# A spectral mixer and a gated feed-forward on one core: the first batch's weight preparation is paced and placed anew

## The chip, the cores and the metric

The kernel runs on one core of a Trainium2 chip. The metric is the device time of one launch in microseconds (us); lower is better. Engines are named as in the profile: PE (matmul), PEld (its weight load), DVE (VectorE), ACT (ScalarE), POOL (GpSimd) and SP (SyncE, which here only issues DMAs).

## What is computed

The input x is (8, 3008, 256). Each batch is filtered along the sequence in the frequency domain and then goes through a gated feed-forward of width 1536.

```python
X = np.fft.rfft(x, axis=1)
Y = X * (filt_r + 1j * filt_i)[None]
y = np.fft.irfft(Y, n=3008, axis=1).reshape(8 * 3008, 256)
g = y @ w_gate
out = (g / (1 + np.exp(-g)) * (y @ w_val)) @ w_out
```

All of it is float32; the gate, value and output weights arrive as float64 and are rounded to float32 on the chip.

## The kernel before

**Spectral part.** The transforms are done as matmuls with tables in stages 1, 2a, 2b and 3, 47 x 64 points at a time. For the first batch all of stages 1 and 2 and the first part of stage 3 run ahead of the feed-forward; for each later batch they run as pieces between the feed-forward's matmuls of the batch before it.

**Feed-forward.** A batch has 8 chunks of tokens (k) and 3 groups of the hidden width (g), so 24 steps. In the first batch the first nine steps go through chunks 0 to 2 for group 0 (steps 0 to 2), then for group 1 (steps 3 to 5), then for group 2 (steps 6 to 8). A fast multiplication scheme works on four blocks: instead of 32 products of blocks, a step has 26. It needs, beside the plain weights P and Q of each block, combined weights A, B and E for each pair of blocks, and sums of the sequence y for distances d = 1, 2, 3 between the blocks (tile `y_t`, function `combine_sequence`). The products land in PSUM as k (L731, tile wk), a and e (wa, we). ACT and DVE turn them into f, c, x, y, m, s, e and h (L746 to L778); POOL forms D = f - f for pairs (L228) and, one step later, sums of h (tokens S). The projections W1 to W7 (L810) of the step before run between the products; o (L225 on DVE, L821 on ACT) adds them up. All three chunks' y are summed for d = 2, 1 and 3 at tokens n2, n1 and n3 of the step before (n3 in the next step).

**Order.** The order is written out by hand: `SCHEDULE` is a list of 150 tokens that each step walks through. The place of a token in it is used in what follows; a step takes about 33 us in the first batch, so a place is worth 0.22 us. Some of the places: S00 and S01 at 5 and 6, x03 20, S10 19, S11 21, s13 22, P0 27, D01 30, A13 31, s01 43, W6 44, D02 48, D12 51, A01 52, c2 53, m01 57, x02 61, W7 62, B01 67, Q3 76, A02 80, A12 87, A23 109, n2 110, E23 123, B23 134, E03 138, n1 139, B03 142. The program keeps this order on each engine (`pin`), and each engine works strictly in its order.

**Preparation of weights.** The class `Preparation` rounds the weights in the first batch. They come as 36 halves, 12 for each group: 8 for the hidden width ("hid") and 4 for the projection ("proj"); halves 8 to 11 are the first group's projection. `round_half` makes nine stages of each: L302, L305, L317 and L321 on DVE, L307 to L314 on ACT, and on POOL a multiplication (L329 for proj, L341 and L342 for hid) and some sums. `combine_weights` makes the combined weights of one pair of blocks in three stages: a sum on DVE (L225, or L232 for d = 1), a scaling on ACT (L363, for d > 1), and then B on POOL (L228) and E on DVE (L225).

Each stage has a tick. Half i starts at tick b, 4 ticks after half i - 1, except half 8, which starts 12 ticks after half 7:

```python
                b = base[-1] + (4 if i != 2 * len(BLOCKS) else 12) if i else 0
                for n, t in enumerate((0, 1, 2, 3, 4, 6, 7, 9, 10)):
                    put(b + t, go, by, n > 6)
```

The combinations follow the last hid half of a group from tick b + 11 on, a pair a tick. Ticks 0 to 28 fall into the spectral part of the first batch. Then `preparation.finish(0)` runs those that step 0 needs, up to tick 44. After that a step runs `TICKS` ticks, evenly spread over its places; step 0 starts behind the token P0. With 22 ticks, step 0 runs ticks 45 to 62, step 1 63 to 84 and step 2 85 to 103. Rounded weights of group 0 go to `wt_t`, of group 1 to `lent`, of group 2 to `wt_t` again.

Ahead of the feed-forward PE runs filler matmuls (`idle`, L463); the last of them read the weights A13 and A01, so they, and with them stage 3 of the first chunk (L639) and step 0, wait for these.

**Other queues.** SP issues the loads of raw weights (L285), of x, t4 and tables (L478), the stores of sums and of y (L937, L934) and the weights' store to DRAM (L371), in the program's order.

Of the kernel before, what the change touches and what calls it, by code (L numbers as in the profile page):

```python
# [84 lines left out]
SCHEDULE = """  # L85
# [14 lines left out]
BLOCKS = (0, 1, 3, 2)  # L100
PAIRS = ((0, 1), (1, 2), (2, 3), (0, 2), (1, 3), (0, 3))
PAIRS_USED = ((1, 3), (0, 1), (0, 2), (1, 2), (2, 3), (0, 3))
# [3 lines left out]
SLOT = {p: i for i, p in enumerate(ORDER)}  # L106
# [38 lines left out]
def kernel(  # L145
# [10 lines left out]
    nc = tc.nc  # L156
# [36 lines left out]
    def weights_of(b, k, g):  # L193
        return wt_1 if b == 0 and k < NT and g == 1 else wt_t
# [27 lines left out]
    pin = tc.keep_in_program_order  # L222

    def add(eng, dst, a, b):
        return eng.tensor_tensor(out=dst, in0=a, in1=b, op=ALU.add)  # L225
# [125 lines left out]
    def combine_weights(g, i, j):  # L351

        d = j - i
        wt_f = weights_of(0, 0, g).rearrange("p s z f -> p s (z f)")
        m = wt_f[:, SLOT[f"A{i}{j}"]]
        ui, uj, yi, yj = [wt_f[:, SLOT[f"{p}{q}"]] for p in "PQ" for q in (i, j)]
        if d == 1:
            pin(negated_sum(m, ui, uj))
        else:
            pin(add(nc.vector, m, ui, uj))  # L360
        yield
        if d > 1:
            pin(nc.scalar.mul(m, m, -1.0 / d))  # L363
        yield
        pin(sub(nc.gpsimd, wt_f[:, SLOT[f"B{i}{j}"]], yi, m))
        pin(add(nc.vector, wt_f[:, SLOT[f"E{i}{j}"]], yj, m))

    def keep_weights(g, piece):

# [7 lines left out]
    class Preparation:  # L377
# [3 lines left out]
        def __init__(self):  # L381
            self.at, self.held = 0, []

            self.ticks, self.need = {}, {}
            base, ready = [], {}

            def put(t, f, by, pool=False):
                self.ticks.setdefault(t, ([], []))[pool].append(f)
                self.need[by] = max(self.need.get(by, 0), t)

            for i, (_, (use, *at)) in enumerate(weights):
                hid, g = use == "hid", at[0] if use == "hid" else at[0] // JB
                by = ((0, 3, 6) if hid else (1, 4, 7))[g]
                b = base[-1] + (4 if i != 2 * len(BLOCKS) else 12) if i else 0
                if i >= N_EARLY:
                    same = [n for n in range(N_EARLY, i) if spot_of(n) == spot_of(i)]
                    k = 2 if spot_of(i) is None else 1
                    last = base[same[-k]] + 8 if same[k - 1:] else 0
                    b = max(b, last + 8)
                    put(max(last, b - 10), lambda i=i: load_weights(i), by)  # L400
                base.append(b)
                if hid and g == NG - 1:
                    ready.setdefault(NT, b)
                half = []

                def go(half=half, i=i):
                    if not half:
                        half.append(round_half(i))
                    next(half[0], None)

                for n, t in enumerate((0, 1, 2, 3, 4, 6, 7, 9, 10)):
                    put(b + t, go, by, n > 6)
                if hid and at[1:] == [BLOCKS[-1], 1]:
                    for n, pair in enumerate(PAIRS_USED):
                        c = combine_weights(g, *pair)
                        for t in range(3):

                            put(b + 11 + n + t, lambda c=c: next(c, None),
                                by if g or n < 4 else 1, t == 2)
            self.barriers = sorted((t, step) for step, t in ready.items())  # L420
            self.end = max(self.ticks)
# [25 lines left out]
                self.tick(step)  # L447

    preparation = Preparation()
    TICKS = 22  # L450

# [385 lines left out]
    with tc.tile_pool(name="start", bufs=1) as spool0:  # L839
# [47 lines left out]
        for u in range(N_TWO + lag):  # L887
            if u < N_TWO:
                spec.turn(u + 2)
                step = spec.stage2a(u)  # L890
# [90 lines left out]
    def chore(step, token, f, *args):  # L981
        chores.setdefault((step, token), []).append((f, args))

    chore(0, "A01", lambda: combine_sequence(cur.y[0], 3))
    for step in range(NT):
        for d, token in ((2, "Q2"), (1, "A01"), (3, "Q3")):
            chore(step, token, keep_sums, step, d)
# [13 lines left out]
    for b in range(B):  # L1001
        cur, nxt = spec, following if b + 1 < B else None
        spec, following = nxt, Spectral(b + 2)
        plan = [[] for _ in range(NCHUNK * NG)]

        def three(s, k, cur=cur):
            return [s.stage3(k, step) for step in range(4)]

        d = [three(cur, k) for k in range(1, NCHUNK)]
        one = [nxt.stage1(u) for u in range(N_ONE)] if nxt else []  # L1010
        two = []
        for u in range(N_TWO + 2) if nxt else ():
            two += [nxt.stage2b(u - 2)] if u > 1 else []
            two += [nxt.stage2a(u)] if u < N_TWO else []
        if nxt:
            plan[0] = one[0:2] + d[0][0:1] + one[2:3] + d[0][1:2]
            plan[1] = one[3:4] + d[0][2:3] + one[4:5] + d[0][3:4] + one[5:6]
            plan[2], plan[3] = one[6:11], one[11:16]
            plan[4] = d[1] + two[0:1]

            plan[5], plan[6] = [iter(())] + two[1:5], two[5:10]
            plan[7] = two[10:11] + d[2]
            plan[8], plan[9] = two[11:16], two[16:21]
            plan[10], plan[11] = two[21:24], three(nxt, 0)
            if b == 0:
                for k in range(NCHUNK - 1):
                    plan[k] = d[k] + one[k:k + 1]
                plan[3], plan[4], plan[5] = one[3:8], one[8:13], one[13:16]
                for n in range(5):
                    plan[6 + n] = two[5 * n:5 * n + 5]  # L1030
                plan[6][0] = sooner(plan[6][0])
        else:
            plan[1], plan[4], plan[7] = d

        for step in range(NCHUNK * NG + (b == B - 1)):
            ghost = step == NCHUNK * NG
            k, g = order_of(b)[min(step, NCHUNK * NG - 1)]
            this = None
            pieces = []
            if not ghost:  # L1040
                pieces = plan[step]
                this = Group(b, k, g, cur.y[k], sequence_of(cur, nxt, step))
                if b == 0:
                    preparation.finish(step)
                chunk = {0: 1, 2: 2, 5: 3}.get(step)
                if b and chunk:
                    for i in range(2):
                        cur.load_t4(chunk, i)
            elif before is None:
                break  # L1050
            ends = {ORDER[e - 1]: n for n, (_, e) in enumerate(PIECES)}
            last = ghost or b == B - 1 and step == NCHUNK * NG - 1
            for place, token in enumerate(SCHEDULE):
                if b == 0 and this and place * TICKS % len(SCHEDULE) < TICKS and \
                        (step or place > SCHEDULE.index("P0")):
                    preparation.tick(step)
                old = token.endswith("'")
                op = token.rstrip("'")
                if op[0] == "t":
                    n = int(op[1])  # L1060
                    ps = pieces_before if old else pieces
                    if n < len(ps):
                        next(ps[n], None)
                elif op[0] in "Wo" or op.endswith(".o"):

                    g0 = older if old else before
                    if g0 is not None and (old or not ghost):
                        g0.project(op)
                else:
                    g0 = before if old else this  # L1070
                    if g0 is not None and not (ghost and op[0] == "S"):
                        g0.step(op)
                if old or this is None:
                    continue
                if nxt and (step, op) == ((4, "P2") if b else (5, "A23")):
                    nxt.load_two(0)
                if b + 2 < B and (step, op) == (9, "B01"):
                    for u in range(2):
                        following.load_x(u)
                if nxt and (step, op) == (10, "A12" if b else "E23"):  # L1080
                    for i in range(2):
                        nxt.load_t4(0, i)
                for f, args in chores.get((step, op), ()) if b == 0 else ():
                    f(*args)
                if op in ends and not last and (b or step >= NT * NG - 1):
                    reload_weights((g + 1) % NG, ends[op])
            older, before, pieces_before = before, this, pieces
# [33 lines left out]
```

## Time and profile before

| | |
|---|---|
| median of 7 runs | 2958.5 us (2957.56 to 2965.78) |
| profiled execution | 2965.28 us, its span 2963.4 us |
| busy: PE, PEld | 99%, 95% of the span |
| busy: DVE, ACT, POOL | 65%, 54%, 53% |
| mean granted clock of TensorE | 0.994 |
| first feed-forward matmul (wk, L731) | at 83.58 us |

The profile's rows are of one execution. PE's share counts a matmul as busy from start to end, so a 99% does not say that it runs at its pace; the number of matmuls (in brackets behind the busy time) in a stretch does, beside the granted clock. A wait is put down to what ended last by the profile.

### The profile page before, as it was taken

The numbers are of one execution on the slowest core, as the hardware profiler recorded it, in microseconds if no ns is written. First come the engines' busy times: TensorE is split into PE (matmuls) and PEld (weight loads), VectorE is DVE, ScalarE is ACT, GpSimd is POOL, SyncE is SP. The second block draws the span as 40 slices with busy tenths as digits, with TensorE's granted clock in tenths as the row PEclk, the third lists the DMA queues.
The fourth block names the chain that finished last, engine by engine and source line by source line (L and its number), as shares of the span: only waits on it lengthen the run. The fifth ranks groups of instructions, "written<-read, shape, count | busy, mean of one in ns | idle before, by whom it ended". The sixth has DMA issues, their size and how long they took to land.

```text
span 2963.4 us, 57624 instructions
## 1 busy us (share of the span) xinstructions
PE 2925.7 (99%) x20264; PEld 2827.8 (95%) x20264; DVE 1932.6 (65%) x4398; ACT 1613.5 (54%) x4208; POOL 1571.0 (53%) x1745
## 2 busy tenths in 40 slices
PE   8999999999999999999999999999999999999999
PEld 6888999999999999999999999999999999999999
DVE  6788765576655766557765567656676566766665
ACT  5765555555555555555555554555555555555554
POOL 3776464555445564446554555544564545555453
PEclk9899999999999999999999999999999999999999
DMA  8577865566555655557555566455665565644442
GB/s 228 179 248 247 279 218 164 186 211 193 176 182 182 220 182 175 188 182 223 184 173 180 185 208 208 156 189 185 201 204 165 182 204 189 206 140 149 147 131 89
DMA packets 217452, 558.57 MB, mean 188 GB/s; under 512 B 29962, under 2 KB 107642, under 8 KB 217166
## 3 DMA queue, kind: packets, MB, share of 16 engines
q1 hardware_dynamic: 171326, 485.59, 52.2%
q10 hardware_dynamic: 36912, 45.43, 4.5%
q0 software_dynamic: 8928, 23.89, 2.3%
q8 instruction: 162, 2.65, 0.4%
q14 instruction: 124, 1.02, 0.1%
HBM read 459.73 MB, written 95.05 MB: 187 GB/s over the span
## 4 chain that ended last, share of the span: by engine, by line
PE 93%; POOL 1%; DVE 1%; ACT 0%; issue 0%; DMA 0%; SPq 0%; POOLq 0%; DVEq 0%; ACTq 0%
PE wa L731 24%; PE wA L810 17%; PE wk L731 16%; PE we L731 12%; PE wG L810 9%; PE wF L810 4%; PE pd L639 3%; PE pa L547 3%; PE pc L619 2%; PE pb L587 2%; POOL y_t L225 1%; POOL h L228 0%; POOL D L228 0%; DMA lent<-in_filt_r_dram 0%; POOL h L225 0%
## 5 line engine op out<-in xcount | busy, mean ns | idle before, releaser
L731 PE MATMUL wa<-y_t,wt_t 128*128 128x188 f32 x4464 | 883.3, 324 | 9.6 <-ACT m L766 3.2
L731 PEld LDWEIGHTS wa<-y_t,wt_t 128*128 128x128 f32 x4464 | 732.4, 191 | 36.1 <-issue 14.7
L225 POOL TENSOR_TENSOR h<-h 128x376 f32<-128x376 f32 x190 | 183.2, 985 | 783.5 <-DVE h L778 783.5
L810 PE MATMUL wA<-wo_t,h 128*128 128x128 f32 x4608 | 577.7, 275 | 2.1 <-DVE o L225 2.1
L810 PEld LDWEIGHTS wA<-wo_t,h 128*128 128x128 f32 x4608 | 563.0, 192 | 15.6 <-issue 11.0
L731 PE MATMUL wk<-y,wt_t 128*128 128x188 f32 x2976 | 568.6, 324 | 0.2 <-ACT f L746 0.2
L228 POOL TENSOR_TENSOR h<-h 128x376 f32<-128x376 f32 x570 | 555.1, 996 | 0.5
L731 PEld LDWEIGHTS wk<-y,wt_t 128*128 128x128 f32 x2976 | 479.8, 191 | 26.6 <-issue 20.8
L228 DVE TENSOR_TENSOR we<-we,m 128x376 f32<-128x376 f32 x576 | 319.0, 556 | 198.4 <-PE we L731 140.8
L731 PE MATMUL we<-y_t,wt_t 128*128 128x188 f32 x2232 | 432.3, 323 | 1.8 <-DVE we L232 1.8
L731 PEld LDWEIGHTS we<-y_t,wt_t 128*128 128x128 f32 x2232 | 369.9, 190 | 2.5 <-DVE we L232 2.2
L228 POOL TENSOR_TENSOR D<-f,f 128x376 f32<-128x376 f32 x288 | 281.0, 989 | 107.2 <-ACT f L746 105.3
L232 DVE SCALAR_TENSOR_TENSOR y<-wk,c 128x376 f32<-128x376 f32 x480 | 245.2, 543 | 135.5 <-ACT we L762 85.0
L766 ACT COPY m<-wa 128x376 f32<-128x376 f32 x576 | 272.2, 473 | 92.2 <-PE wa L731 90.9
L773 ACT ACTIVATE g<-wa 128x188 f32<-128x188 f32 x576 | 188.2, 327 | 192.1 <-PE wa L731 184.0
L810 PE MATMUL wG<-wo_t,h 128*128 128x128 f32 x2304 | 289.5, 276 | 0.6 <-DVE o L225 0.6
L810 PEld LDWEIGHTS wG<-wo_t,h 128*128 128x128 f32 x2304 | 282.7, 192 | 0.8 <-DVE o L225 0.8
L773 ACT ACTIVATE u<-we 128x188 f32<-128x188 f32 x576 | 189.2, 329 | 167.6 <-DVE we L228 148.2
L746 ACT ACTIVATE f<-wk 128x376 f32<-128x376 f32 x288 | 139.4, 484 | 240.5 <-PE wk L731 212.5
L750 ACT COPY c<-wk 128x376 f32<-128x376 f32 x288 | 136.2, 473 | 225.6 <-PE wk L731 225.3
L753 DVE SCALAR_TENSOR_TENSOR x<-wk,f 128x376 f32<-128x376 f32 x192 | 104.5, 545 | 234.5 <-PE wk L731 230.2
L762 ACT COPY we<-y 128x376 f32<-128x376 f32 x480 | 223.5, 486 | 31.0 <-DVE h L778 12.3
(142 smaller groups left out, 3922.2 us busy)
## 6 DMA issues: line engine op xcount, KB each, us to landing
wt_t<-w_all SPq DMA_DIRECT2D x174, 896.0 KB
wt_t<-w_all SPq DMA_DIRECT2D x174, 768.0 KB
t<-d SPq DMA_DIRECT2D x62, 384.0 KB
d<-t ACTq DMA_DIRECT2D x112, 192.0 KB
lent<-de_tbl SPq DMA_DIRECT2D x84, 256.0 KB
lent<-in_filt_r_dram SPq DMA_DIRECT2D x336, 64.0 KB
lent<-d SPq DMA_DIRECT2D x84, 256.0 KB
d<-lent ACTq DMA_DIRECT2D x84, 256.0 KB
```

What stands on the lines that cost most here:

```text
L225: return eng.tensor_tensor(out=dst, in0=a, in1=b, op=ALU.add)
L228: return eng.tensor_tensor(out=dst, in0=a, in1=b, op=ALU.subtract)
L232: return nc.vector.scalar_tensor_tensor(out=dst, in0=a, scalar=-1.0, in1=b, op0=ALU.mult, op1=ALU.subtract)
L547: pin(nc.tensor.matmul(out=ps[0:NK], lhsT=wf_t, rhs=self.x.pop(u), start=True, stop=True))
L731: pin(nc.tensor.matmul(out=ps[:, z], lhsT=self.wt[:, SLOT[p], z], rhs=rhs, start=start and z == 0, stop=True, skip_group_check=True))
L746: pin(act.mul(self.small(f"f{i}", f"f{i}", 1), t[f"k{i}"], -1.0))
L750: pin(act.copy(out=self.small(f"c{i}", f"c{i}", 1), in_=t[f"k{i}"]))
L753: pin(v.scalar_tensor_tensor(out=dst, in0=t[f"k{j}"], scalar=-1.0, in1=t[f"f{i}" if j == 3 else f"D{at}"], op0=ALU.mult, op1=ALU.add))
L762: pin(act.copy(out=self.bank(f"e{at}"), in_=t[f"y{at}"]))
L766: pin(act.copy(out=self.small(f"m{at}", "m", 4), in_=t[f"a{at}"]))
L773: pin(act.activation(out=self.small(op, "g", 3, 1)[:, 0], in_=ps[:, 1], func=AF.Silu))
L810: pin(nc.tensor.matmul(out=self.tiles[at][:, t, :], lhsT=self.hs[i][:, HID[p], t0:t0 + 128], rhs=wo_t[:, JB * q + i, WO[p], :], start=star ...
```

## The change

Five places change, and all of them act on the first batch alone:

- the sum that makes E runs on DVE only for the first four pairs of group 0, which are those made ahead of the feed-forward; for the other two pairs of group 0 and for all six of groups 1 and 2 it runs on POOL, behind the same pair's B;
- half 8 starts 8 ticks after half 7 instead of 12, and all later halves 4 ticks nearer with it;
- a step runs 20 ticks instead of 22;
- in step 0 the ticks start behind A01 instead of P0;
- the sums of the sequence for d = 3 of the first chunk are made behind B01 instead of A01.

With this, step 0 runs ticks 45 to 57 (tick 58 is run by `finish` as step 1 begins), step 1 ticks 59 to 78, step 2 ticks 79 to 98. The combinations of group 1 (ticks 91 to 98) stand at places 90 to 143 of step 2, where before (95 to 102) they stood at 69 to 116. Those of group 2 (139 to 146) stand at places 0 to 53 of step 5, where before (143 to 150) they stood at place 116 of step 4 to place 14 of step 5.

```diff
         pin(sub(nc.gpsimd, wt_f[:, SLOT[f"B{i}{j}"]], yi, m))
-        pin(add(nc.vector, wt_f[:, SLOT[f"E{i}{j}"]], yj, m))
+        early = g == 0 and PAIRS_USED.index((i, j)) < 4
+        pin(add(nc.vector if early else nc.gpsimd, wt_f[:, SLOT[f"E{i}{j}"]], yj, m))
...
-                b = base[-1] + (4 if i != 2 * len(BLOCKS) else 12) if i else 0
+                b = base[-1] + (4 if i != 2 * len(BLOCKS) else 8) if i else 0
...
-    TICKS = 22
+    TICKS = 20
...
-    chore(0, "A01", lambda: combine_sequence(cur.y[0], 3))
+    chore(0, "B01", lambda: combine_sequence(cur.y[0], 3))
...
                 if b == 0 and this and place * TICKS % len(SCHEDULE) < TICKS and \
-                        (step or place > SCHEDULE.index("P0")):
+                        (step or place > SCHEDULE.index("A01")):
                     preparation.tick(step)
```

## The prediction

> **What bounds the kernel now.** I read the page's busy rows first, then the stretches by engine, then the waits of the stretches that stand out, then their instructions in order of time.
>
> ```profile
> span 2963.4 us, 57624 instructions
> PE 2925.7 (99%) x20264; PEld 2827.8 (95%) x20264; DVE 1932.6 (65%) x4398; ACT 1613.5 (54%) x4208; POOL 1571.0 (53%) x1745
> ```
>
> TensorE is busy 99% of the span: nothing on another engine counts unless it makes PE wait or its clock drop. So I look for the places where PE is not at its pace. In the stretches the columns are length, then busy us (instructions) of PE, PEld, DVE, ACT, POOL, then granted clock, DMA share, GB/s.
>
> ```profile
> 72.70:86.40 13.70, 13.22 (x48) 11.15 (x49) 7.64 (x15) 5.21 (x10) 5.46 (x7) 0.50 0.46 111
> 93.20:96.60 3.40, 1.54 (x8) 1.25 (x8) 2.67 (x8) 2.36 (x9) 2.63 (x4) 0.99 0.36 122
> 96.60:103.40 6.80, 6.55 (x24) 6.58 (x25) 5.65 (x14) 4.71 (x14) 3.31 (x7) 0.50 0.47 139
> 117.00:150.00 33.00, 32.48 (x233) 30.80 (x232) 26.43 (x64) 25.20 (x70) 28.25 (x38) 1.00 0.67 231
> 171.70:175.10 3.40, 1.72 (x12) 1.27 (x10) 2.56 (x8) 2.94 (x9) 1.71 (x3) 1.00 0.69 279
> 175.10:181.90 6.80, 5.45 (x21) 5.45 (x22) 6.65 (x18) 4.44 (x13) 4.57 (x7) 0.50 0.34 79
> 249.00:260.00 11.00, 7.94 (x52) 6.96 (x51) 10.97 (x19) 5.76 (x16) 9.75 (x10) 1.00 0.80 268
> ```
>
> A smooth stretch runs 233 matmuls in 33.0 us, 7.06 per us. The stretch from 96.6 runs 24 in 6.8 us at half clock, where 48 would go: 3.4 us lost. That from 175.1 runs 21 (3.0 us of work): 3.8 lost, of which 1.35 is idle and the rest clock. Both follow 3.4 us in which PE was busy only about half the time. After 400 us hardly anything is lost, so all that the change can win or lose lies in the first batch. Feed-forward step 0 starts at 83.6 us, step 2 at about 151, step 5 at 248 and step 6 at 282. Who is waited for (us in total, times, longest), in four windows: 91 to 97 (step 0), 168 to 177 (step 2), 254 to 259 (step 5), 290 to 295 (step 6):
>
> ```profile
> PE wa L731 <- POOL y_t L225: 1.4, 1, 1.4
> PE wa L731 <- DVE wa L753: 1.3, 1, 1.3
> ...
> PE wa L731 <- ACT m L766: 2.8, 2, 1.6
> PE we L731 <- DVE we L232: 1.8, 1, 1.8
> DVE w L302 <- POOL lent L225: 1.3, 1, 1.3
> ...
> PE wa L731 <- DVE wa L753: 2.5, 1, 2.5
> ...
> DVE wa L753 <- POOL D L228: 2.8, 1, 2.8
> PE wA L810 <- DVE o L225: 1.1, 1, 1.1
> ```
>
> The first row names the last of several releasers. The product that waited was B01; its sums on POOL had ended at 88.8, and what ended just ahead of it (96.71) was ACT's copy m01, behind two scalings of the d=3 sums and a rounding step. So DVE and ACT are the late ones, both in strict order, with rounding work between the feed-forward's own.
>
> ```profile
> L225 DVE TENSOR_TENSOR lent<-lent x9: 410/413/943, 164.5 to 180.8; 128x256 f32<-128x256 f32 x9
> L228 POOL TENSOR_TENSOR lent<-lent x6: 726/752/904, 168.6 to 178.0; 128x256 f32<-128x256 f32 x6
> ```
>
> One weight sum costs 0.41 us on DVE, 0.94 when POOL runs beside it, and 0.75 on POOL (duration min/median/max).
>
> **The change part by part.** Written as us against the profiled execution, minus is gain.
>
> *First projection half 4 ticks nearer, ahead of the feed-forward.* Ticks 36 to 44 run before it. They now hold eight more rounding instructions: on DVE L317 and L321 of half 8, L305 of half 9 and L302 of half 10; on ACT all four of half 9. The load of half 12 moves ahead of x loads on SP, not needed before 112 us: nothing. What counts is the order: two DVE stages (L302, L305) and three on ACT (L307, L310, L312) now stand ahead of the sum and scaling that make weight A13, and a filler matmul ahead of stage 3 waits for A13. Now: DVE sum at 70.58, ACT scaling to 71.45, PE goes on at 71.55. Then: DVE 0.3 to 0.5 + 0.3 to 0.8, ACT L310 and L312 0.5 each, scaling 0.42: A13 at 72.6 to 73.3. PE is at half clock from 72.7, so stage 3 and step 0 start later by 0.5 to 2.2: **+1.6**, because the two filler matmuls then also run at half pace. The rest of the added work lies in DVE's idle 77.8 to 80.4 and ACT's 75.7 to 81; if stage 3 came sooner it would cost up to 2.
>
> *No ticks until A01, d=3 sums at B01.* Between P0 and A01 DVE loses L305, L317, L321, L302 and two weight sums (0.73+0.95+0.74+0.28 and 1.20+0.41), ACT four stages and a scaling. The subtraction for A01 (L753, at 93.27) then waits only for c0, g0 and D01 and can run at about 90.8; A01 on PE moves from 93.86 to 92.1 behind f2 and P2. Copy m01 loses the two scalings (0.34 each) ahead of it: B01 from 96.85 to about 94. That is the 2.9 of the two waits and ACT's 0.2: **-2.9** (bounds -1 and -3.5). What is late next is f2 itself. On SP the store of the d=3 sums (issued at 96.78) goes some 3 us later and holds the loads of t4 behind it (98.06), which stage 3 reads at 116: nothing. With PE busier before 96.6 the half-clock stretch after it may go: 3.4, less what ACT and DVE then can't follow: **-2.5** (0 to -3.4).
>
> Here I weigh the Trainium skill, "TensorE: Matmul & The Clock Gate", section "Why this matters for your kernels": it asks for no gaps over about 3 us between bursts. In the rows no gap near 96.6 or 175.1 is over 2.0 us, and the clock fell; a window half idle sufficed. By the rule both clock gains are zero and the sum below is 5.0 smaller; I take the trace.
>
> *Last half of the first group: 20 ticks, later start.* The multiply of half 11 (L329, tick 57, one more in the catch-up) now stands on POOL behind the d=1 sums at n1, with half 10's behind the d=2 sums. POOL runs from 107.93 without a gap; 3.4 (d=2) + 0.7 + 4.4 (d=1) + 0.7 ends at 117.1, and W2's matmul, which waits for it, now starts at 116.0 behind DVE: **+1.1** (0 to +4: a 2 us gap may pull the clock). S00 and S01 stand behind it, and their readers come 9 us later.
>
> *Twelve later sums plus two of the first group on POOL.* In step 2 DVE loses six sums (0.41 to 0.94, some 3.3 us in all), POOL gains 6x0.75 = 4.5. Two more things help: L302 of half 22, which waited 1.3 us for POOL to free its buffer, now stands 8 places (1.8 us) further behind that POOL add, and the combinations start at place 90 of 150 instead of 69. The waits there sum to 4.6: **-3.5** (-1 to -5). The half clock at 175.1: **-2.5** (0 to -3.4). In return POOL has 12 sums, 2 multiplies and 4 subtractions (12x0.7+1.4+2.0 = 11.8 us) from place 105 on, with 10 us left of the step: about 2 us spill over S00: **+0.7** (0 to +3).
>
> *Third group.* Its combinations move from the end of step 4 into places 0 to 53 of step 5. Ahead of x03 DVE has five instructions instead of eight, four of them sums of 0.94 to 1.22: the 2.5 wait goes: -2.7. But POOL must do ten sums (7.0) beside S10, S11, D01, S20, S21 (5x1.0) before D02: from 251.7 it is done at 264.8, where x02 would be due at 261.1. DVE stands at x02 for 3.7 us, with y12, y02, h13 and o behind it. PE needs that first at A02, due at 266.0: **+1.5** (0 to +5, at 0.8 and 1.1 us apiece). Step 6: D01 loses the four subtractions (1.8) ahead of it: -1.3; but six rounding stages on DVE instead of two fall beside the second batch's stage 2: +1.0.
>
> Against this stands "GPSIMD Engine Reference", section 4.1: elementwise adds belong on VectorE, GpSimd being about twice as slow for two inputs. The quiet rows agree (0.75 against 0.41). By it twelve sums cost 9 us to free 5, and the third group's part would be +1.5 alone. But DVE's own sums at 249.7 to 255.7 took 1.16, 0.94, 1.22 and 1.20 beside POOL, so there the trade is even, and I take these.
>
> Sum: 1.6-2.9-2.5+1.1-3.5-2.5+0.7-2.7+1.5-1.3+1.0 = **-9.5**. The profiled execution took 2965.3 (its span and 1.9 around it), 6.8 above the median of 2958.5; the seven runs differ by 8.2, about two half-clock stretches. A median run probably has fewer of these, so I count half of the clock gain, 2.5 less: -7.0, **2951.5**.
>
> **The rivals.** (A) Forecast: fewer waits. 2943 to 2956.
> (B) Gains and costs cancel: the clock drops anyway somewhere else, since a new window half idle (the wait for W2's weights, 2.1 us) replaces the old. Then -9.5 + 5.0 + 2 = -2.5: 2956. For: PE waits of 1 us remain at 109. Against: step 2's waits have a clear cause that goes.
> (C) Slower: POOL becomes the bound in step 5. At 0.9 per sum and 1.15 per S and D, D02 ends at 267.6; A02 waits 2.7 us, which is over the 2.0 that went with a drop, 3.4 more, and W2 pays the same (+3.4). With the clock gains gone, only 1.5 won in step 2 and its spill at 3: 1.6-2.9+1.1+3.4-1.5+3-2.7+6.1-0.3 = +7.8: 2966. It decides from D02 ending after 265. For: POOL is 28.25 of 33 busy in step 1 already. Against: POOL's weight sums pair at 0.7.
> (D) The change does little, as the steps are bound by PE: 2958. Against: 20 us are visibly lost.
>
> **How the numbers follow.** A 0.57, B 0.20, C 0.17, D 0.06. 0.2% is 5.9 us, about what a measurement of this kernel can tell from no change. A gives faster in 0.9 of its cases; B and D are mostly within; C is slower in most. Faster 0.54, within 0.27, slower 0.19. A's own range is 2943 to 2957; to leave out 2 in 10 it is drawn from 2943 to 2964.
>
> **What would show it.** Right: first wk matmul about 1.6 later; no PE wait over 0.5 between A01 and B01; clock 1.00 from 96 to 103 and around 175; W2's second matmul released by L329; no wait at x03 in step 5, DVE waiting at L753 x02 for POOL's D. Wrong: PE waits over 2 us at A02 of step 5, a half-clock stretch near the start of step 1 or 5, or waits of 1 us and more left in step 2.

## The result, and the profile after

The changed kernel takes 2948.6 us (median of 11 runs, 2947.3 to 2951.85) where the kernel before takes 2958.3 beside it (29 runs, 2955.65 to 2966.13): 9.7 us less, a ratio of 0.9965 with an interval of 0.9957 to 0.9973. It is faster, by more than the 0.2% that can be told from no change. The forecast was 2951.5.

The profiled execution of the changed kernel took 2951.85 us, the longest of its 11. Its lines from L366 on stand one further than in the kernel before (L731 is L732, L753 is L754, L778 is L779, L810 is L811). The page's busy rows:

```profile
span 2949.6 us, 57623 instructions
PE 2915.1 (99%) x20264; PEld 2817.2 (96%) x20264; DVE 1930.7 (65%) x4384; ACT 1611.8 (55%) x4208; POOL 1579.9 (54%) x1759
```

PE is still busy 99%, with the same 20264 matmuls; DVE has lost 14 instructions and POOL has gained 14, which are the moved sums (two of group 0, six each of groups 1 and 2). The gain is in the stretches where PE was not at its pace. Columns as in the forecast: length, then busy us (instructions) of PE, PEld, DVE, ACT, POOL, granted clock, DMA share, GB/s.

```profile
72.70:86.40 13.70, 13.70 (x82) 11.05 (x81) 9.80 (x20) 8.49 (x18) 8.16 (x9) 0.90 0.58 170
96.60:103.40 6.80, 5.40 (x32) 4.59 (x32) 6.55 (x18) 6.55 (x19) 4.20 (x6) 1.00 0.74 198
106.20:109.60 3.40, 0.81 (x8) 0.68 (x7) 3.40 (x9) 1.96 (x6) 3.32 (x5) 1.00 0.89 348
109.60:113.00 3.40, 3.40 (x18) 3.40 (x17) 0.22 (x2) 0.45 (x1) 3.40 (x6) 0.50 0.76 267
169.40:176.20 6.80, 5.52 (x35) 4.99 (x36) 6.49 (x15) 4.18 (x12) 5.44 (x8) 1.00 0.75 246
248.00:259.00 11.00, 10.08 (x63) 8.47 (x62) 9.45 (x22) 6.03 (x17) 10.70 (x13) 1.00 0.48 158
```

Ahead of the feed-forward the clock is low for one stretch of 3.4 us (from 72.0), not for all of 13.7. From 96.6 and around 175 it is full now. In their place there is one new low stretch, from 109.6, behind 3.4 us in which PE ran 8 matmuls. Who PE waits for, in step 0 and the head of step 1 (84 to 118), in step 2 and the head of step 3 (151 to 187) and in step 5 (246 to 283); each row gives us in total, times and longest:

```profile
PE wF L811 <- POOL wo_t L329: 2.6, 1, 2.6
PE wa L732 <- issue: 1.4, 1, 1.4
PE wa L732 <- ACT m L767: 1.2, 2, 1.0
...
PE wF L811 <- DVE h L779: 1.5, 1, 1.5
PE we L732 <- ACT we L763: 1.4, 1, 1.4
...
DVE x L754 <- POOL D L228: 1.6, 1, 1.6
PE wA L811 <- DVE o L225: 1.1, 2, 0.9
PE wA L811 <- POOL wt_t L225: 0.5, 1, 0.5
```

The first row is W2 at the head of step 1, which waits for the multiply of half 11. The waits for DVE's `wa` and for m in step 2 are gone, and so is the 2.5 at x03 in step 5; there DVE now waits for D02, which stands behind POOL's sums. The sums in step 2 (forms by shape, 151 to 176.2: count, busy us, mean ns):

```profile
L228 POOL TENSOR_TENSOR lent<-lent 128x256 f32<-128x256 f32 x6 | 4.9, 814 | 3.3 <-ACT lent L363 3.3
L225 POOL TENSOR_TENSOR lent<-lent 128x256 f32<-128x256 f32 x6 | 4.7, 787 | 0.0
L225 DVE TENSOR_TENSOR lent<-lent 128x256 f32<-128x256 f32 x3 | 2.2, 733 | 0.0
```

DVE kept three of nine sums there; POOL took six at 0.79 us each, near the 0.75 of the forecast.

The lengths of the steps, from the first W matmul of one (`wF` in the trace) to that of the next, in us; step 0 begins with the first `wk`:

| | first wk at | step 0 | 1 | 2 | 3 | 4 | 5 | 6 | 7 to 9 | end |
|---|---|---|---|---|---|---|---|---|---|---|
| before | 83.6 | 31.4 | 33.1 | 40.4 | 30.2 | 30.2 | 32.1 | 32.6 | 92.5 | 2963.4 |
| after | 80.0 | 25.9 | 37.1 | 33.1 | 32.0 | 30.2 | 30.5 | 31.9 | 91.6 | 2949.6 |
| after, second profile | 77.4 | 26.4 | 35.2 | 33.0 | 32.0 | 30.2 | 30.4 | 31.9 | 91.5 | 2945.3 |

Everything behind takes 2557.2 us in all three. The whole difference is made in the first ten steps and ahead of them.

### The profile page after: what moved, and what is told of

Same layout as the page of the kernel before. It is cut to its first block, busy times and chain, and to the rows that moved or that the text cites. A ratio compares the mean times of both kernels' runs of the same rounds, so it can differ in the third digit from the quotient of the medians.

```text
span 2949.6 us, 57623 instructions
## 1 busy us (share of the span) xinstructions
PE 2915.1 (99%) x20264; PEld 2817.2 (96%) x20264; DVE 1930.7 (65%) x4384; ACT 1611.8 (55%) x4208; POOL 1579.9 (54%) x1759
## 4 chain that ended last, share of the span: by engine, by line
PE 94%; DVE 1%; POOL 1%; ACT 0%; issue 0%; DVEq 0%
PE wa L732 24%; PE wA L811 17%; PE wk L732 16%; PE we L732 12%; PE wG L811 9%; PE wF L811 4%; PE pd L640 3%; PE pa L548 3%; PE pc L620 2%; PE pb L588 2%; POOL wt_t L225 0%; POOL wt_t L228 0%; DVE o L225 0%; POOL h L228 0%; DVE h L779 0%
## 5 line engine op out<-in xcount | busy, mean ns | idle before, releaser
L732 PE MATMUL wa<-y_t,wt_t 128*128 128x188 f32 x4464 | 880.4, 323 | 4.3 <-issue 1.4
L732 PEld LDWEIGHTS wa<-y_t,wt_t 128*128 128x128 f32 x4464 | 730.0, 190 | 29.9 <-issue 17.6
L811 PE MATMUL wA<-wo_t,h 128*128 128x128 f32 x4608 | 577.9, 275 | 3.0 <-DVE o L225 2.0
L811 PEld LDWEIGHTS wA<-wo_t,h 128*128 128x128 f32 x4608 | 562.8, 192 | 17.1 <-issue 10.6
L732 PE MATMUL wk<-y,wt_t 128*128 128x188 f32 x2976 | 567.5, 323 | 0.0
L732 PEld LDWEIGHTS wk<-y,wt_t 128*128 128x128 f32 x2976 | 479.0, 190 | 25.7 <-issue 20.2
L732 PE MATMUL we<-y_t,wt_t 128*128 128x188 f32 x2232 | 431.6, 323 | 1.4 <-ACT we L763 1.4
L732 PEld LDWEIGHTS we<-y_t,wt_t 128*128 128x128 f32 x2232 | 369.4, 190 | 1.8 <-ACT we L763 1.7
L811 PE MATMUL wG<-wo_t,h 128*128 128x128 f32 x2304 | 288.3, 275 | 0.6 <-DVE o L225 0.6
L811 PEld LDWEIGHTS wG<-wo_t,h 128*128 128x128 f32 x2304 | 281.4, 192 | 0.8 <-DVE o L225 0.8
L754 DVE SCALAR_TENSOR_TENSOR x<-wk,f 128x376 f32<-128x376 f32 x192 | 104.5, 545 | 235.9 <-PE wk L732 229.8
L763 ACT COPY we<-y 128x376 f32<-128x376 f32 x480 | 224.1, 487 | 33.7 <-DVE h L779 15.3
```

The source lines that it names most:

```text
L732: pin(nc.tensor.matmul(out=ps[:, z], lhsT=self.wt[:, SLOT[p], z], rhs=rhs, start=start and z == 0, stop=True, skip_group_check=True))
L754: pin(v.scalar_tensor_tensor(out=dst, in0=t[f"k{j}"], scalar=-1.0, in1=t[f"f{i}" if j == 3 else f"D{at}"], op0=ALU.mult, op1=ALU.add))
L763: pin(act.copy(out=self.bank(f"e{at}"), in_=t[f"y{at}"]))
L811: pin(nc.tensor.matmul(out=self.tiles[at][:, t, :], lhsT=self.hs[i][:, HID[p], t0:t0 + 128], rhs=wo_t[:, JB * q + i, WO[p], :], start=star ...
```

## The experiments

**One part of the change alone.** Each is the kernel before with one edit. They ran together, beside a kernel before of 2958.76 (33 runs).

```diff
only_sums: E's sum on DVE only for the first four pairs of group 0, else on POOL
-        pin(add(nc.vector, wt_f[:, SLOT[f"E{i}{j}"]], yj, m))
+        early = g == 0 and PAIRS_USED.index((i, j)) < 4
+        pin(add(nc.vector if early else nc.gpsimd, wt_f[:, SLOT[f"E{i}{j}"]], yj, m))
only_start:
-    chore(0, "A01", lambda: combine_sequence(cur.y[0], 3))
+    chore(0, "B01", lambda: combine_sequence(cur.y[0], 3))
...
-                        (step or place > SCHEDULE.index("P0")):
+                        (step or place > SCHEDULE.index("A01")):
only_rate:
-    TICKS = 22
+    TICKS = 20
only_near:
-                b = base[-1] + (4 if i != 2 * len(BLOCKS) else 12) if i else 0
+                b = base[-1] + (4 if i != 2 * len(BLOCKS) else 8) if i else 0
```

> Before with the engine of the late E sums alone changed (POOL). If DVE's load is what costs in steps 2 and 5: 4 to 7 us faster than before (2951 to 2954), the waits of 4.6 us in step 2 mostly gone; step 5 gains its 2.5. If POOL becomes the bound: slower by 2 us or more, with DVE at the L753 of x02 waiting for D. If the whole change works only by fewer ticks: 0 +- 1.

> Before with step 0's ticks behind A01 and the d=3 sums at B01 alone. If rounding ahead of A01 holds up ACT and DVE: the waits of 2.9 us near A01 and B01 go and 3 to 5 us are won (2953 to 2955). But the first group's last half then ends later still (ticks 45 to 58 in step 0, the rest in a burst before step 1): a burst of 4 ticks before step 1 may cost 2 to 4 and leave 0 to +2.

> Before with 20 ticks a step alone. If spacing alone eases POOL and DVE: 1 to 3 us faster, since the buffer wait of L302 in step 2 goes (1.3 and what follows). If lower pace only delays the first group's projection: 0 to 2 slower, as tick 60 to 62 come in a burst at step 1.

> Before with half 8 four ticks nearer alone. If the eight more instructions ahead of the feed-forward delay A13: 0.5 us at the filler matmul, and step 0 keeps its waits: 0 to +2 slower. If ending the first group's projection 4 ticks sooner counts by itself: 1 to 2 faster.

Measured: sums 2954.98 (ratio 0.9987, 0.9977 to 0.9996), start 2958.58 (1.0000, 0.9991 to 1.0009), rate 2957.65 (0.9997, 0.9988 to 1.0006), near 2960.7 (1.0007, 0.9998 to 1.0016). Only the sums are a gain by themselves, and they fall short of the 4 to 7 that were expected of them: step 5 wins 2.2, but step 2's waits stay. Of the start the second case came true, nothing in all; the rate's 1.1 and the nearer half's cost of 1.9, in the range given for it, are not clear of no change. The four differences are -3.8, -0.2, -1.1 and +1.9: together -3.2, a third of the 9.7.

**One part undone.** Each is the changed kernel with one of the same edits taken back; they ran together, beside 2959.47 (31 runs). Three of the texts on record describe an edit wrongly. What un_sums does is to put every sum for E back on DVE, as before. In those for un_start and un_rate the "sums" that begin at P0, or come 22 to a step, are ticks, and the moved sums that "stay" are on POOL, not on VectorE. Their numbers stand.

> The change with its first part undone: the first batch's four d=1 sums of weights go back to GpSimd, ahead of the feed-forward of the second batch; the start of the later sums, the rate and the nearer half stay changed. Theory 1 (step 2's gain is made by the sums on VectorE, and by nothing else): the waits of TensorE in step 2 for weights that VectorE rounds late (about 3 to 5 us) come back, and the half-clock stretch near 175 with them: 4 to 6 us slower than the changed kernel, that is 2953 to 2955 us. Theory 2 (the lower rate and the later start have given GpSimd the room, and the sums on VectorE are no longer needed): within 2 us of the changed kernel.

> The change with its second part undone: GpSimd's sums of later weights begin at P0 again and the d=3 sums at A01. Theory 1 (the start past A01 takes the waits of step 0 away, whatever else is changed): TensorE's waits between A01 and B01 come back, 3 us, and where they fall in one window a half-clock stretch of 3.4 to 6.8 us behind them: 4 to 6 us slower than the changed kernel, 2953 to 2955 us. Theory 2 (the start alone was worth nothing when it was the only edit, because what is not summed early is summed in a burst ahead of step 1; the same holds here): within 1.5 us of the changed kernel, with the wait of step 1's first matmul for GpSimd gone or under 1 us.

> The change with the rate undone: 22 sums of later weights a step in place of 20; the sums on VectorE, the later start and the nearer half stay. Theory 1 (the rate is worth the waits of step 5 and little else, 1 us as the only edit): 1 to 2 us slower than the changed kernel, 2949.5 to 2950.5 us. Theory 2 (the lower rate puts the last half of W2's weights behind GpSimd's d=1 sums at the end of step 0, and so makes the 2.6 us wait at the head of step 1 and the half-clock stretch behind it): that wait goes, and the sum is nil or 1 to 2 us faster than the changed kernel, 2946.5 to 2948.5 us.

> The change with the nearer half undone: half 8 of the feed-forward's weights stands 12 behind again, not 8. Theory 1 (the nearer half costs as part of the change what it cost as the only edit, 2 us, by the later start of the first projection): 1 to 2 us faster than the changed kernel, 2946.5 to 2947.5 us. Theory 2 (it is what makes the later start pay: without it GpSimd has one more half to sum when it may begin only past A01, and the last halves are late at step 1): the wait at the head of step 1 grows from 2.6 to 4 us or more, 2 to 4 us slower than the changed kernel, 2950.5 to 2952.5 us.

Measured: un_sums 2956.95 (0.9994, 0.9984 to 1.0004), un_start 2954.85 (0.9985, 0.9977 to 0.9994), un_rate 2953.05 (0.9978, 0.9969 to 0.9988), un_near 2952.38 (0.9977, 0.9967 to 0.9987). Against their own kernel before that is -2.5, -4.6, -6.4 and -7.1. From -9.7, undoing a part costs 7.2, 5.1, 3.3 and 2.6. By the medians every part is needed, even the nearer half, which alone cost 1.9; for the last two the interval overlaps that of the change. So un_near went as its theory 2 had it (the wait is 5.1) and un_start by 5.1 as its theory 1, though W2's wait shrank too, as its theory 2 had it. un_rate lost W2's wait for POOL, as theory 2 said, and still was slower by more than theory 1's 1 to 2: in its profile, which is the longest of its runs, steps 2 and 6 cost more than step 1 gave. un_sums cost more than theory 1's 4 to 6, and elsewhere: its step 2 stayed at 33.9. The parts don't add; why, the step lengths show (one profile each, us from half clock in brackets where there is any):

| kernel | first wk at | step 0 | 1 | 2 | 3 | 5 | 6 |
|---|---|---|---|---|---|---|---|
| before | 83.6 | 31.4 (10) | 33.1 | 40.4 (7) | 30.2 | 32.1 | 32.6 |
| only_sums | 80.1 | 30.8 (10) | 33.2 | 40.1 (7) | 30.2 | 29.9 | 32.6 |
| only_start | 78.0 | 26.6 | 36.7 (3) | 38.2 | 30.2 | 33.7 (3) | 32.6 |
| only_rate | 78.0 | 30.0 (7) | 33.9 | 37.4 (7) | 30.2 | 34.2 (3) | 31.8 |
| only_near | 78.5 | 29.2 (3) | 33.6 | 42.1 (7) | 30.2 | 32.1 | 32.6 |
| un_sums | 77.9 | 27.7 | 36.7 (7) | 33.9 | 31.7 | 33.7 (3) | 31.9 |
| un_start | 77.9 | 31.8 (10) | 33.0 | 36.6 | 30.4 | 31.7 | 32.0 |
| un_rate | 85.6 | 26.0 (1) | 33.4 | 38.2 | 30.2 | 29.9 | 34.2 (3) |
| un_near | 78.2 | 26.0 | 39.2 (7) | 33.1 | 32.0 | 30.5 | 31.9 |
| start_rate (below) | 78.2 | 26.7 | 39.9 (7) | 34.0 | 31.7 | 34.8 (3) | 31.9 |
| after | 80.0 | 25.9 | 37.1 (3) | 33.1 | 32.0 | 30.5 | 31.9 |

Step 0 is short (26 to 28) wherever the start is late and 29 or more elsewhere. With the start undone, A01 waits again for the subtraction on DVE, and half clock follows from 87.9 on; PE's waits from 76 to 120:

```profile
PE wa L732 <- DVE wa L754: 2.5, 1, 2.5
PE wF L811 <- POOL y_t L228: 1.3, 1, 1.3
PE wa L732 <- POOL y_t L225: 1.3, 1, 1.3
```

Step 1 pays for it. The last half of W2's weights comes late; the nearer half pulls it forward, the lower rate pushes it back. W2's wait in only_start, un_near and un_rate, in this order (84 to 118; in un_rate POOL is not waited for at all):

```profile
PE wF L810 <- POOL wo_t L329: 4.5, 1, 4.5
```

```profile
PE wF L811 <- POOL wo_t L329: 5.1, 1, 5.1
```

```profile
PE wF L811 <- DVE h L779: 1.1, 1, 1.1
```

So the nearer half halves that wait, 5.1 to 2.6: alone it has no such wait to shorten. Its cost alone is in step 2 (42.1), where PE waits for DVE for 4.5 us (141 to 187):

```profile
PE wa L731 <- DVE wa L753: 4.5, 2, 3.1
```

Step 5 depends on the sums: with them on DVE (un_sums) and the rate at 20, PE waits at x03 for 2.8 us and a low stretch follows it (246 to 283); in the kernel before it was 2.5, with no stretch behind it. The row names no releaser, but DVE's subtraction for that product ends at 251.8 and PE goes on at 251.9. With only the sums moved, this wait is not there, and DVE waits for POOL instead (240 to 262):

```profile
PE wa L731 <- issue: 2.8, 1, 2.8
```

```profile
DVE x L754 <- POOL D L228: 1.4, 1, 1.4
```

Step 2 goes to 33 or 34 us in just those kernels that have both the late start and the rate of 20, whether the sums are moved (33.1) or not (33.9). That was not what the forecast had held, so the pair was built alone (below). The waits of step 2, though, change with the rate alone: PE's in only_start, which are close to those of the kernel before, and in only_rate (142 to 179 in both):

```profile
PE wa L731 <- ACT m L766: 3.0, 3, 1.6
PE we L731 <- DVE we L232: 1.8, 1, 1.8
PE we L731 <- ACT we L762: 0.6, 1, 0.6
...
PE we L731 <- ACT we L762: 1.9, 2, 1.4
PE wa L731 <- POOL lent L228: 0.4, 1, 0.4
PE wF L810 <- DVE h L778: 0.2, 1, 0.2
```

The place at which the combinations of group 1 begin in step 2 follows from the ticks (with 22, step 2 of the kernel before runs ticks 85 to 106, not to 103). Over all kernels PE's idle time in that step (its length less PE's busy time) goes with it:

| place | kernels | PE idle in step 2, us |
|---|---|---|
| 41 | only_near | 7.4 |
| 69 | before, only_start, un_rate; only_sums | 5.6 each; 4.9 |
| 75 | un_start | 3.8 |
| 90 | only_rate; start_rate, un_sums; un_near, after | 2.7; 2.5 each; 1.9 each |

So it is the later place that takes these waits away, and there the moved sums take 0.6 more. The rate alone moves the place from 69 to 90; with the nearer half it takes the late start as well. It also tells what the nearer half costs alone: it pulls the combinations forward to place 41.

**Late start and rate together**, the kernel before with the edits of only_start and only_rate.

> The kernel before with two parts of the change: the later start in step 0 (behind A01, the d=3 sums behind B01) and 20 ticks a step. Theory 1 (it is these two together, and not the sums of weights on GpSimd, that clear step 2; each of them alone left it at 37 to 38 us): step 2 takes 33 to 34.5 us, without a half-clock stretch near 171; step 0 takes 26 us; step 1 about 39 us, by the wait for half 11; step 5 keeps its wait at x03 (32 to 34 us). From the step lengths of the kernels with one part and with one part undone the whole is 2954 to 2956.5 us, 2.5 to 4.5 under the kernel before, where the two parts alone sum to 1.3. Theory 2 (the sums on GpSimd clear step 2): step 2 stays at 36 us or more, and the whole is at 2957 us or above.

Measured: 2957.75, beside 2958.06 (0.9997, 0.9988 to 1.0006). The steps came out as theory 1 had them: step 2 at 34.0 with no low stretch near 171, step 0 at 26.7, step 1 at 39.9, step 5 at 34.8. The total did not: it is above the 2954 to 2956.5 that was expected of it, in the range of theory 2, and no gain that could be measured. Steps 0 and 2 win 4.7 and 6.4 over the profile of before; steps 1, 3 and 5 give back 6.8, 1.5 and 2.7. The two waits that eat it (84 to 118 and 246 to 283):

```profile
PE wF L810 <- POOL wo_t L329: 5.1, 1, 5.1
...
PE wa L731 <- issue: 2.8, 1, 2.8
```

What the start adds in step 2 is not a wait. In only_rate and start_rate the instructions of DVE, ACT and POOL in that step stand in the same order, and PE has the same three waits of 0.4, 0.6 and 1.4 us. But a low stretch of 6.8 us begins in the last of them in only_rate, which is the 3.4 us between 37.4 and 34.0, and there is none in start_rate. Cut into windows of 3.41 us on the grid on which each profile's low stretches lie, this is what the two look like (only_rate, then start_rate):

```profile
166.66:170.07 3.41, 1.79 (x9) 1.23 (x8) 3.41 (x9) 0.83 (x2) 0.87 (x2) 1.00 0.91 299
170.07:176.90 6.83, 6.06 (x16) 4.95 (x17) 6.75 (x19) 4.89 (x14) 3.66 (x5) 0.50 0.40 141
...
167.74:171.15 3.41, 2.37 (x17) 1.92 (x16) 3.41 (x8) 1.73 (x4) 1.26 (x2) 1.00 0.99 265
171.15:174.57 3.42, 2.07 (x10) 1.45 (x10) 3.42 (x8) 1.96 (x6) 2.16 (x3) 1.00 0.78 308
```

In only_rate 1.6 us of the waits fall into one window, in start_rate 1.0 and 1.4 into two. That the later place takes away step 2's waits is shown; that the start takes away its low stretch was seen in one profile of each kernel, and may be a matter of where the grid lay.

That is how the four parts hang together. The start clears step 0, and with the rate it puts step 2's combinations at place 90; together they make W2's wait and leave the one in step 5. Moving the sums takes away the one in step 5: from start_rate to un_near, -0.3 to -7.1. The nearer half takes away half of the one in step 1: from un_near to after, -7.1 to -9.7.

**The rest of W2's wait.** The changed kernel, with step 0 alone at 22 ticks. Half 11's multiply then stands at place 137, ahead of the sums at n1.

```diff
-                if b == 0 and this and place * TICKS % len(SCHEDULE) < TICKS and \
+                rate = TICKS if step else 22
+                if b == 0 and this and place * rate % len(SCHEDULE) < rate and \
```

> The changed kernel with one thing different: step 0 alone keeps the rate of 22, so that the last multiply of half 11 (L329) stands at place 137, ahead of GpSimd's d=1 sums at n1, and not behind them at the start of step 1; steps 1 and later stay at 20. Theory 1 (the 2.6 us wait of TensorE for this multiply at the head of step 1, and the half-clock stretch of 3.4 us behind it, come from that place alone): the wait is under 0.5 us, step 1 takes 33 to 34 us in place of 37.1, step 2 stays near 33, and the whole is 2 to 4 us faster than the changed kernel: 2944.6 to 2946.6 us. Theory 2 (the multiply is late because GpSimd has too much to do in step 0, wherever it stands): the wait moves to the d=1 sums or to S00 and the time is within 1 us of the changed kernel. Theory 3 (the tick more in step 0 brings the ticks of step 2 one place forward and its waits of 1 to 2 us back): step 1 gains 3.5, step 2 loses 3 to 5, and the whole is the same or slower.

Measured: 2947.7 (6 runs, 2946.92 to 2955.66), beside 2958.06 (0.9970, 0.9958 to 0.9981). The multiply starts at 103.7 instead of 107.9, and PE does not wait for it; the two records of L329 in the changed kernel and in this one (98 to 115), then PE's first wait in this one (84 to 118):

```profile
L329 POOL TENSOR_TENSOR wo_t<-wo_t,pw x1: 959/959/959, 107.9 to 107.9; 128x256 f32<-128x256 f32 x1
```

```profile
L329 POOL TENSOR_TENSOR wo_t<-wo_t,pw x1: 782/782/782, 103.7 to 103.7; 128x256 f32<-128x256 f32 x1
```

```profile
PE wF L811 <- DVE h L779: 1.5, 1, 1.5
```

Step 1 is 33.8 and step 2 33.6, as theory 1 had them. But the time is 0.9 under the changed kernel's earlier median, not 2 to 4, and the intervals overlap. That is theory 2's number, without its mechanism. So both were run side by side.

> The changed kernel once more, for a second profile of it and side by side with the next kernel. Theory 1 (the wait for half 11 at the head of step 1 is there in every execution, but a half-clock stretch follows it only in some, as its first profile was the longest of 11 executions): the wait is again 2 to 3 us, step 1 takes 35 to 35.5 us without a half-clock stretch near 110, or 37 with one, and the median is 2948 to 2949.5 us. Theory 2 (the stretch always follows): step 1 takes 37 us again, and the median is 2 to 4 us above the next kernel's.

> The changed kernel with the rate of 22 in step 0 alone, once more, on the same chip as the changed kernel. Theory 1 (only the wait itself is saved in most executions, 1 to 1.5 us, because TensorE then waits 1.5 us for h anyway): median 0.5 to 1.5 us under the changed kernel's in the same call, step 1 under 34 us in the profile. Theory 2 (the saved half-clock stretch counts in full): 2 to 4 us under it.

Measured: after 2948.2 (5 runs, 0.9965, 0.9952 to 0.9977), with 22 ticks in step 0 2948.37 (6 runs, 0.9963, 0.9951 to 0.9975), beside 2959.9. No difference; both expectations for the second missed. In these two profiles step 1 falls from 35.2 to 33.7, while steps 0 and 2 and steps 7 to 9 grow by 0.2, 0.6 and 0.4. PE waits 1.5 us for h in any case, so only 1.1 of the 2.6 was to be had. The wait was there again in the second profile of after (2.6), and so was a low stretch, from 107.1. PE going on behind the wait in the first and in the second profile, then the stretch in the second:

```profile
108.93 1.94 PE L811 MATMUL wF<-wo_t,h 128*128 128x128 f32 x10 [2.59 <-POOL wo_t L329]
106.76 2.18 PE L811 MATMUL wF<-wo_t,h 128*128 128x128 f32 x10 [2.58 <-POOL wo_t L329]
107.10:110.50 3.40, 3.40 (x19) 3.40 (x18) 0.55 (x2) 0.00 (x0) 3.32 (x6) 0.51 0.76 264
```

In both the stretch lies behind the wait, over work, and costs the same: the wk matmuls at 115.3 and 113.1 start 6.4 us after the wait's end in both. Still step 1 took 35.2 in the second and 37.1 in the first. What differs is one instruction of DVE, a rounding stage at the head of step 1 (L317 at 115.1 in the first, at 113.0 in the second), and the waits of PE that follow it in the first alone (118 to 127):

```profile
L317 DVE SCALAR_TENSOR_TENSOR pw<-wo_t,pw x1: 3969/3969/3969, 115.1 to 115.1; 128x256 uint32<-128x256 uint32 x1
L317 DVE SCALAR_TENSOR_TENSOR pw<-wo_t,pw x1: 720/720/720, 113.0 to 113.0; 128x256 uint32<-128x256 uint32 x1
...
PE wa L732 <- DVE wa L754: 0.5, 1, 0.5
PE wA L811 <- ACT o L822: 0.5, 1, 0.5
PE wa L732 <- ACT m L767: 0.2, 1, 0.2
```

So neither theory had it: the stretch followed in both profiles, as theory 2 said, and step 1 took theory 1's 35 to 35.5 with it.

## Why the prediction was right, point by point

The sum against its own profile was -9.5, the forecast for the median -7.0, measured -9.7 between the medians and -13.8 between the two profiles. The runs bear out the forecast's main case, fewer waits and less half clock in the first steps. Not all of its own signs came, though. The clock around 96 and 175, W2's releaser and x02 in step 5 were as said; the start did not come later, and B01 still waits. Two of the three signs of being wrong are there as well, a half-clock stretch near the start of step 1 and a wait of 1.4 us in step 2; both were small beside the gain. By steps, in us, from the two profiles of the changed kernel:

| step of the prediction | forecast | first profile | second profile |
|---|---|---|---|
| start of the feed-forward (half 8) | +1.6 | -3.6 | -6.2 |
| step 0: no ticks until A01, half clock at 96.6 | -2.9 - 2.5 | -5.5 | -5.0 |
| step 1: W2 behind POOL's sums | +1.1 | +4.0 | +2.1 |
| step 2: waits, half clock at 175.1 | -3.5 - 2.5 | -7.3 | -7.4 |
| spill into step 3 | +0.7 | +1.8 | +1.8 |
| step 5: x03, then D02 | -2.7 + 1.5 | -1.6 | -1.7 |
| step 6 | -1.3 + 1.0 | -0.7 | -0.7 |

**Start of the feed-forward.** The delay of A13 is not what sets it: over the kernels the first `wk` is at 77.4 to 78.5 in the executions with no low stretch ahead of it, with the nearer half or without (only_start 78.0, un_sums 77.9). One stretch of 3.4 us makes it 80.0 to 80.5, and 13.7 us of half clock make it 83.6 in before and 85.6 in un_rate, which has the nearer half. This last pair differs by 2.0, close to the 1.6 that was reckoned for half pace. In a usual execution the term is nil. un_rate's profile from 72.5:

```profile
72.50:86.20 13.70, 12.71 (x41) 9.60 (x42) 9.40 (x19) 6.09 (x14) 4.67 (x7) 0.50 0.49 125
```

Such executions stand at the long end of their kernel: un_rate's 11 runs fall into five of 2950.6 to 2951.7, two of 2953.0 to 2953.6 and four of 2956.9 to 2958.8, and the profiled one took 2958.83; of before's 29 runs four lie at 2965.7 to 2966.1, near its profiled one (2965.28), and all others under 2962.

**The discount was the term mis-sized.** The profiled execution of before lay 6.8 above its median, and from this half of the clock gain was taken off. But most of that excess fits the 13.7 us ahead of the feed-forward (first `wk` at 83.6, not 78), which the sum didn't count at all; the stretches at 96.6 and 175.1 are there in other executions too (10 and 7 us in only_sums, whose steps 0 and 2 are about as long as before's). The granted clock says the same: its mean is 0.9969 over the 33 runs of before beside the kernels with one part, and 0.9985 over 11 of after. The share that is missing from 1, times the run's time, is at most 9.2 us before and 4.6 after (at most, since low clock costs nothing while PE is idle). So of the 10.2 us between the two means, 2959.0 and 2948.8, up to 4.6 is clock and the rest waits. The sum had 5.0 and 4.5. Undiscounted, -9.5 was the better number, though that it comes within 0.2 of the measured -9.7 is luck: it holds the 1.6 of the start, which is nil in a usual execution, and steps 1 and 3 were forecast 2.1 to 4.0 us too low together.

**Step 0** came out as said in size, but not in its parts. Step 0 before and after:

```profile
83.58:114.98 31.40, 27.49 (x143) 25.58 (x142) 23.83 (x56) 22.03 (x62) 22.17 (x26) 0.85 0.44 137
79.99:105.92 25.93, 22.95 (x144) 20.88 (x142) 21.21 (x49) 20.26 (x57) 22.00 (x26) 1.00 0.54 167
```

PE's idle time fell only from 3.9 to 3.0, where 2.9 was forecast. A01's wait went from 1.25 to 0.40; but B01 still waits 1.0 for m01, where less than 0.5 was expected, and a wait of 1.4 at 100.5 is new. The other 4.5 goes with the clock, where 2.5 was forecast: half clock before was 6.8 us from 96.6, and in this execution 2.8 more at the end of the stretch ahead of the feed-forward. That the sum fits is luck. un_start, with a step 0 of 31.8, shows that the late start does it.

**W2** was the right place with the right releaser: a wait of 2.6, where rival B had named 2.1. That "a 2 us gap may pull the clock" stood only in the bound (+4), and the clock was pulled in both profiles. The step that failed is taking +1.1, the wait alone, as the value. The wait and the stretch together made +2.1 in the second profile; the +4.0 of the first holds the slow L317 besides.

**Step 2** was right in its size and wrong in its author. The forecast put the gain on the sums that DVE loses, and named the later places of the ticks as "two more things". The runs show the reverse: the later places take away the waits without the sums (PE idle in step 2 for 5.6 us before, 2.7 in only_rate), the sums alone leave 40.1, and on top of start and rate they give 0.9. The forecast's term for the clock came true in the profile, but the same waits with and without a low stretch (only_rate and start_rate, before and only_start) make it a matter of the single execution and not a sure gain.

**Step 3**'s spill came, but W waits for h on DVE (1.5), not for POOL's S00.

**Step 5** went as said: x03's wait went with the sums, DVE stands at x02 for POOL's D. It stands there for 1.6, not 3.7, since x02 came due 13.6 us into the step and not 12.2, and D02 ended at 15.1 and not 15.9 (253.6 in a step that now begins at 238.5). PE loses 1.1 and 0.5 at W matmuls and nothing at A02. Rival C, POOL as the bound in step 5, needed D02 after 265, which is 16.1 us into the step; it came within 1.0 of that, but the waits at A02 and the low stretch did not appear. Of rival B one thing came true, a new half-idle window in place of an old one, at W2.

Against the Trainium skill, "GPSIMD Engine Reference", section 4.1, which would have the sums on VectorE, the trace was the better guide here: moved alone they are worth 3.8 us, on top of start and rate 6.8. The forecast gives the range of its main case once to 2956 and once to 2957; the measured 2948.6 is in both.

## What to carry to other kernels

Preparation work that is spread over a schedule moves its waits about: clear one step, and look at once for the step in which the last of that work is now late. Judge the parts of such a change together and by the length of each step, since a part that loses alone can be what makes another pay. And before a profile's excess over the median is discounted from a gain, find where in the profile that excess lies. A low-clock stretch in one profile belongs to that execution first; look whether another kernel with the same waits has it too.

## What the runs showed of the hardware

**The clock.** The low clock comes in stretches of 3.4 us or multiples of it (3.4, 6.8, 10.2, 13.7). The Trainium skill, "TensorE: Matmul & The Clock Gate", section "Part 1: The HAM clock gate", says that activity is judged in windows of about 3.4 us that run free of the kernel; the runs agree in the length and in that a window's edges fall differently against the same waits. An idle window, as the page has it, was not needed: PE had run 8 matmuls in the 3.4 us ahead of the stretch at 109.6, and no gap there was over 2.6 us. The same wait can come with or without a stretch, as in step 2 of only_rate and start_rate, and again in step 5: PE waits 2.5 us for DVE in the kernel before and in only_start. On each profile's grid (before, then only_start):

```profile
253.57:256.99 3.42, 2.41 (x19) 2.12 (x17) 3.42 (x4) 2.97 (x8) 3.42 (x4) 1.00 1.01 333
256.99:260.40 3.41, 1.89 (x10) 1.63 (x11) 3.38 (x8) 0.79 (x2) 2.38 (x3) 1.00 0.78 266
...
245.85:249.27 3.42, 1.06 (x7) 0.77 (x5) 3.42 (x5) 1.64 (x5) 3.06 (x4) 1.00 1.01 328
249.27:252.68 3.41, 3.25 (x9) 2.93 (x10) 2.89 (x8) 0.80 (x2) 1.38 (x2) 0.50 0.49 176
```

Split over two windows the wait leaves PE busy for 2.41 and 1.89 us, and the clock holds; nearly whole in one it leaves 1.06, and the clock falls. Over all fourteen profiles, from 60 to 330 us, PE was busy for at most 0.53 of the window ahead of each stretch. Every window at full clock with less than 0.41 was followed by one; between 0.41 and 0.53 both happened. The stretch of 13.7 us ahead of the feed-forward fits this: in the profiles of before and un_rate PE was busy for 0.40 and 0.38 of the window ahead of it. Why it then lasted four windows, where 0.41 in after and 0.08 in rate22_step0 brought only one, was not settled; the long one is in none of the other twelve.

**A DVE instruction beside POOL.** L317 at the head of step 1 took 3.97 us in the first profile of after and 2.87 in start_rate; no other DVE instruction in the fourteen profiles took over 2 us. Both ended 0.3 us behind the end of an unbroken run of POOL's instructions (at 118.8 and 120.5). Why it was held in these two and not in the others stays open.
